# Fills of a long rest counted at full clock, and later loads in halves, in a linear-attention and MoE kernel

## The chip, the core and the metric

The kernel runs on one core of one Trainium2 chip. The metric is the device time of one execution in microseconds (us). Before the change three executions took 614.2, 611.24 and 614.52 us, with a median of 614.2 us.

## What is computed

A delta-rule attention over 768 time steps (4 batches, 8 heads, head size 48) feeds a gated two-layer product with no nonlinearity but the product of its two halves. `w_a` and `w_b` are 384 x 1536, `w_out` is 1536 x 384, and 3072 tokens go through them:

```python
for t in range(S):
    y[:, :, t] = einsum('bhd,bhde->bhe', q[:, :, t], state)
    v_old = einsum('bhde,bhd->bhe', state, k_n[:, :, t])
    state = state + beta[:, :, t] * einsum('bhd,bhe->bhde', k_n[:, :, t], v[:, :, t] - v_old)
x = y.transpose(0, 2, 1, 3).reshape(B * S, H * D)
out = ((x @ w_a) * (x @ w_b)) @ w_out
```

## The kernel before

**Tiling.** The 768 steps are 24 chunks of 32. Four chunks are a group: `prep` loads the chunks' rows, forms norms and the 32 x 32 products of keys and queries, `solve` inverts a triangular system for each head on VectorE (pairs of a multiply into `tmp` and a subtraction from `b`), and `steps` takes each chunk through the state: products named W and X (only where the inverse is made in two halves, group 0), K, U, A and the state's update S. Two chunks give one token block `s` of 256 tokens, which goes through the MoE product in twelve units, one for each block of 128 of the 1536 columns (`moe`, `moe_out`). The first two token blocks use float32 weights (`FULL = 2`), the other ten use float16 pairs.

**Weights.** The twelve weight blocks come packed as 64-bit words, 1152 KB each, by `load(b, "w")` on SyncE's queue. `decode(b)` turns one into float32 with three VectorE instructions of 128 x 1152. Blocks 0, 1 and 2 are loaded at the start. The rest, along with the raw rows (`r`, 1024 KB for two chunks, into `rawb` or `late`), the keys (`k`, `knb`) and values (`v`, `vnb`, 384 KB each), come after the first attention output of chunk 1. The buffers of the packed blocks are `late`, two halves of `stage`, and for blocks 3 to 5 a part of `wt` that is not yet used.

**How later loads are held back.** `over` is a list of one-element places. Once chunk 1's `u` is computed, each load first gets a one-element copy on GpSimd, from the place two entries back in `over` into the buffer that the load will fill. The copy cannot run before the load two back has landed, and the load cannot be issued before the copy. So two loads are in flight. The list takes loads until it has `THROTTLE` entries, 18 before. Later loads are issued as soon as their buffer is free.

**What sets the order.** Nothing is in the order in which it is written: `Plan` records every instruction as an operation, `link` finds the dependences, and `pack` lays out each engine's program with a price for each instruction, a due time for TensorE's work (`slot`, `when`), a model of TensorE's clock, and one of how its instructions are fetched. Every engine then runs its own program strictly in that order.

**Fills.** Where `pack` sees TensorE resting it adds matmuls on constants into a spare bank, whose result nobody reads, so that the clock stays up. In a rest over `LONG` (4 us) they are four-pass float32 matmuls of 128 x 512 (`self.idle[1]`, `ones`), after up to 40 tiny ones (`burn`), otherwise bfloat16 ones (`self.idle[0]`, `wide`). Before the change a fill was counted at double length where the model took the clock to be low, and in a long rest none was placed in its last 1.5 us (`SLACK`). In the profile the tiny ones are line 528, the other fills line 532, and everything else of the plan is line 541.

Of the kernel before, what the change touches and what calls it, by code (L numbers as in the profile page):

```python
# [12 lines left out]
F32 = mybir.dt.float32  # L13
F32R = mybir.dt.float32r
F16 = mybir.dt.float16
I32 = mybir.dt.int32
# [6 lines left out]
B, H, S, D = 4, 8, 768, 48  # L23
# [3 lines left out]
P = 128  # L27
# [22 lines left out]
def slot(c, piece):  # L50
    if piece == "G" and c < 4:
        v = -30 + 0.1 * c
    elif c < 2:
        v = {
            0: {"W": -20, "X": -19, "U": -17, "A": -13.1, "S": 1.0},
            1: {"W": -15.2, "X": -14, "K": -15, "Q": -11.1, "U": -13, "A": -11, "S": 2.0},
        }[c].get(piece, -30)
    elif c < 4 and piece != "G":
        v = {
            2: {"W": 2.5, "X": 3.2, "K": 3.8, "U": 4.6, "S": 5.2, "A": 5.8},  # L60
            3: {"W": 6.2, "X": 6.8, "K": 7.4, "U": 8.2, "A": 9.0, "S": 9.8},
        }[c].get(piece, -30)
    elif piece == "G":
        v = 5.0 + 2.2 * (c - 4) if c < 8 else finish(c // 4 * 4 - 4 + c % 4 // 2) - 0.5 + 0.1 * (c % 2)
    else:
        v = finish(c) - {"W": 7, "X": 6.5, "K": 5.5, "U": 4.0, "S": 3, "A": 1.5}[piece]
    return when(v)
# [3 lines left out]
LAG = 2  # L71
THROTTLE = 18
PADS, WARM = 40, 4
# [11 lines left out]
class Plan:  # L85
# [93 lines left out]
    def price(eng, name, outs, ins, kw):  # L179
        out = outs[0]  # L180
# [17 lines left out]
        if eng == "ACT":  # L198
            extra = 93.0 * (hasattr(kw.get("scale"), "tensor") + ("accum_out" in kw))
            if name == "copy" and out.dtype == F16 and wide and wide[0].dtype == F16 and out.shape[0] == 32:  # L200
                extra += 105.0
            if name == "copy" and psum and out.shape[0] == 32 and len(out.shape) == 4:
                extra += 110.0
            if name == "copy" and wide and not psum and len(wide[0].shape) == 3 and abs(wide[0].ap[-1][0]) > 4:
                extra += 225.0
            return (50 if psum else 93) + n / 1.2 + extra
        if eng == "DVE":
            speed, extra = 1.0, 61.0 * (n > 1 and any(a.shape[-1] == 1 and len(a.shape) == 2 for a in ins))
            if name == "tensor_reduce":
                n = 1  # L210
                for d in ins[0].shape[1:]:
                    n *= d
            elif name == "tensor_copy" and out.dtype == F16 and wide and wide[0].dtype == F16:
                speed, extra = 4.0, 95.0
            elif name.startswith("tensor_scalar") and not psum:
                speed = 2.0
            elif name == "memset":
                speed = 1.0 if out.dtype == F32 else 2.0
            elif name == "reciprocal":
                extra = 167.0  # L220
            return (66 + n / speed) / 0.96 + extra
# [92 lines left out]
    def pack(self, pri, back=False):  # L314
# [18 lines left out]
        while len(done) < n:  # L333
# [66 lines left out]
            if e == "PE" and not back:  # L400

                if kept and t > self.SINCE:
                    f = max(free[e], self.SINCE)
                    wide = t - f > self.LONG
                    stop_, burn, many = t - self.SLACK * wide, 0, 0

                    def spend(f, many, words, brief):
                        nonlocal until, warm, use, pos, edge, come, then
                        while True:
                            while until <= f:  # L410
                                warm = use > 0.43 * self.WINDOW if warm else use > 0.75 * self.WINDOW
                                use, until = 0.0, until + self.WINDOW
                            idle.words, idle.dur = words, brief if warm else 2 * brief
                            step = self.stall(idle, f, pos, edge, come, then)
# [6 lines left out]
                    if wide:  # L421
# [8 lines left out]
                        else:  # L430
                            burn = 0
                        many = spend(f, 0, 4, 871.0)
                    else:
                        many = spend(f, 0, 2, 218.0)
                    fill[i] = burn, many, wide
                while until <= t:
# [37 lines left out]

    START, MOVE = 900.0, (1100.0, 400.0)
    BLOCK, EDGE, FETCH, BUSY, FIRST, AHEAD, STALL, PEEK = 256, 193, 4100.0, 2500.0, 1000.0, 30, 250.0, 2
    SINCE, UNTIL, LONG, SLACK = 10000.0, 40e3, 4000.0, 1500.0
    ENTER, LEAVE, STICK = 210.0, 10.0, 15e3
# [43 lines left out]
    def issue(self, tc):  # L522
        with tc.manual_schedule():
            for i in self.order():
                burn, many, wide = self.fill.get(i, (0, 0, False))
                for n in range(burn):
# [3 lines left out]
                    )  # L530
                for _ in range(many):
                    self.nc.tensor.matmul(
                        self.pool[-1],
                        self.idle[wide],
                        self.idle[wide].unsqueeze(1).broadcast_to([P, 4, P]),
                        start=True,
# [8 lines left out]
def tile_kernel(ctx, tc, kqt, kqs, kn, vn, beta, w, masks, picks, out):  # L545
# [268 lines left out]

    def goal(c, what):
        if what == "w":
            a = place(c).bitcast(F32)
        elif what == "t":
            a = turned(c)
        elif what == "r":  # L820
            return rawp(c)[0:1, 0, 0:1]
        else:
            return (knp if what == "k" else vnp)(c)[0:1, 0, 0:1]
        return a[0:1, 0:1]

    def load(c, what):
# [3 lines left out]
        if over and what != "s" and len(over) < THROTTLE:  # L830
            dst = goal(c, what)
            G.tensor_copy(dst, over[max(0, len(over) - 2)])
            over.append(dst)
        plan.behind = set(hold)
# [694 lines left out]
```

## Time and profile before

| | |
|---|---|
| three executions | 614.2, 611.24, 614.52 us |
| the profiled execution | 614.43 us, of which the profile's span is 612.7 us |
| TensorE busy (matmuls) | 595.0 us, 97% of the span |
| VectorE, ScalarE, GpSimd busy | 404.4, 302.1, 35.5 us |
| moved by DMA | 46.46 MB, 44.85 MB of it on SyncE's queue |
| chain that ended last | 72% TensorE, 18% VectorE, 6% ScalarE |

The profile is one execution. PE is TensorE's matmuls, PEld its weight loads, DVE VectorE, ACT ScalarE, POOL GpSimd, SPq the issue of a DMA by SyncE. A row of the timeline has the start, the time taken, engine, line, operation, the tiles (out<-in), the shape and the count, and in brackets the idle time of the engine before it with what ended that. A float32 matmul shows as two instructions, so x12 is one unit's six. PEclk is the share of the full TensorE clock that was granted.

### The profile page before, as it was taken

The numbers are of one execution on the slowest core, as the hardware profiler recorded it, in microseconds if no ns is written. First come the engines' busy times: TensorE is split into PE (matmuls) and PEld (weight loads), VectorE is DVE, ScalarE is ACT, GpSimd is POOL, SyncE is SP. The second block draws the span as 40 slices with busy tenths as digits, with TensorE's granted clock in tenths as the row PEclk, the third lists the DMA queues.
The fourth block names the chain that finished last, engine by engine and source line by source line (L and its number), as shares of the span: only waits on it lengthen the run. The fifth ranks groups of instructions, "written<-read, shape, count | busy, mean of one in ns | idle before, by whom it ended". The sixth has DMA issues, their size and how long they took to land.

```text
span 612.7 us, 25247 instructions
## 1 busy us (share of the span) xinstructions
PE 595.0 (97%) x11465; PEld 466.7 (76%) x11465; DVE 404.4 (66%) x1093; ACT 302.1 (49%) x756; POOL 35.5 (6%) x49
## 2 busy tenths in 40 slices
PE   7699998999989999999999999999999999999997
PEld 4477776777768787877787778787777778777875
DVE  5869886998899845699653996553995344244222
ACT  4212323598763753564655357445356545535322
POOL 1012230001100100000101000101000000000000
PEclk9889999999999999999999999999999999999999
DMA  6718698000411204203013013010000000000000
GB/s 219 270 67 320 229 349 292 28 0 3 154 60 53 71 7 149 59 21 129 4 59 122 4 33 118 3 33 24 4 27 3 3 28 2 3 27 3 27 1 26
DMA packets 11931, 46.46 MB, mean 76 GB/s; under 512 B 1328, under 2 KB 4784, under 8 KB 8752
## 3 DMA queue, kind: packets, MB, share of 16 engines
q1 hardware_dynamic: 11824, 44.85, 20.8%
q8 instruction: 89, 1.46, 1.0%
q14 instruction: 18, 0.15, 0.1%
HBM read 40.13 MB, written 4.72 MB: 73 GB/s over the span
## 4 chain that ended last, share of the span: by engine, by line
PE 72%; DVE 18%; ACT 6%; issue 2%; DMA 1%; SPq 0%; ACTq 0%
PE bank L541 60%; PE duo L541 10%; DVE b L541 6%; DVE tmp L541 4%; PE S_ps L541 3%; ACT wt L541 2%; DVE g L541 2%; DVE wt L541 1%; ACT sqf L541 1%; DMA rawb<-in_kqt 1%; DVE ghl L541 1%; DVE f L541 1%; ACT a L541 1%; DVE n L541 1%; ACT sqy L541 1%
## 5 line engine op out<-in xcount | busy, mean ns | idle before, releaser
L541 PE MATMUL bank<-xb,wt 128*128 128x256 f16 (+1 forms) x1800 | 247.3, 291 | 2.9 <-issue 2.5
L541 PEld LDWEIGHTS <-wt 128*128 128x128 f16 x2160 | 208.1, 98 | 35.8 <-issue 1.0
L541 DVE TENSOR_TENSOR g<-bank,a 128x256 f32<-128x256 f32 x144 | 60.4, 420 | 125.3 <-ACT a L541 124.3
L541 PE MATMUL bank<-wt,ghl 128*128 128x384 f16 x720 | 136.6, 326 | 0.0
L541 ACT ACTIVATE a<-bank,gs 128x256 f32<-128x256 f32 x120 | 56.8, 473 | 119.1 <-PE bank L541 118.7
L541 PEld LDWEIGHTS <-ghl 128*128 128x128 f16 x720 | 67.6, 98 | 35.1 <-issue 0.4
L541 ACT CAST ghl<-g 128x256 f16<-128x256 f32 x120 | 48.3, 403 | 59.3 <-DVE g L541 58.7
L541 PE MATMUL bank<-stage,wt 128*128 128x256 f16 x648 | 76.7, 273 | 0.0
L541 DVE TENSOR_TENSOR ghl<-g,ghl 128x256 f16<-128x256 f32 x120 | 51.2, 427 | 33.8 <-ACT ghl L541 33.3
L541 PEld LDWEIGHTS bank<-xb,wt 128*128 128x128 f32 x288 | 53.4, 190 | 13.6 <-issue 3.1
L541 DVE TENSOR_TENSOR b<-b,tmp 128x31 f32<-128x31 f32 (+20 forms) x170 | 56.3, 331 | 3.4
L541 DVE TENSOR_TENSOR tmp<-b,b 128x31 f32<-128x31 f32 (+20 forms) x170 | 56.2, 331 | 3.3
L541 ACT COPY y<-duo 32x384 f32<-32x384 f32 x88 | 41.4, 470 | 2.5 <-PE duo L541 1.4
L541 PE MATMUL bank<-wt,g 128*128 128x384 f32 x96 | 37.5, 502 | 0.0
L541 DVE TENSOR_TENSOR f<-vnb,duo 128x768 f32<-128x768 f32 (+1 forms) x23 | 21.4, 929 | 5.8 <-issue 4.2
L541 POOL TENSOR_TENSOR vnb<-vnb,nm 128x384 f32<-128x384 f32 x20 | 17.8, 910 | 125.2 <-DMA vnb<-in_vn 104.8
L541 ACT COPY u<-duo 128x768 f32<-128x768 f32 (+1 forms) x23 | 18.1, 785 | 10.7 <-PE duo L541 10.2
L541 PEld LDWEIGHTS duo<-sh,rawb 48*64 48x64 f32 x1152 | 18.4, 134 | 5.9 <-issue 4.2
L541 ACT ACTIVATE sqy<-y 128x96 f32<-128x96 f32 x80 | 22.3, 278 | 0.9
L541 ACT COPY a<-bank 128x256 f32<-128x256 f32 x24 | 8.9, 369 | 26.4 <-PE bank L541 26.3
L541 PEld LDWEIGHTS duo<-f,tt 32*32 32x32 f32 x1408 | 16.4, 105 | 6.9 <-issue 3.6
L541 PEld LDWEIGHTS bank<-wt,g 128*128 128x128 f32 x96 | 16.9, 189 | 6.0
(156 smaller groups left out, 617.4 us busy)
## 6 DMA issues: line engine op xcount, KB each, us to landing
rawb<-in_kqt SPq DMA_DIRECT2D x10, 1024.0 KB, 5.2
stage<-in_w SPq DMA_DIRECT2D x6, 1152.0 KB, 7.3
vnb<-in_vn SPq DMA_DIRECT2D x12, 384.0 KB, 4.6
out<-ob SPq DMA_DIRECT2D x24, 192.0 KB, 1.9
knb<-in_kn SPq DMA_DIRECT2D x10, 384.0 KB, 3.9
stage<-in_kqs SPq DMA_DIRECT2D x8, 448.0 KB, 3.8
late<-in_w SPq DMA_DIRECT2D x3, 1152.0 KB, 5.8
wt<-in_w SPq DMA_DIRECT2D x3, 1152.0 KB, 6.7
```

The source lines that it names most:

```text
L541: fn(*(self.place(a, lease) for a in args), **{k: self.place(a, lease) for k, a in kw.items()})
```

## The change

It has three parts. In a long rest the fills are now counted at one length whatever the modelled clock, they may reach to 0.3 us before the next work, and a remainder is given to short fills; short rests keep 150 ns free. The loads that `over` holds back come, for weights and raw rows, as two DMAs of half the columns, each half with its own copy on GpSimd and its own entry in `over`, and the list goes up to 33 entries, so that two halves are in flight. And some numbers of the planner change: two prices, one due time, one DMA constant.

```diff
@@ -58,7 +58,7 @@
     elif c < 4 and piece != "G":
         v = {
             2: {"W": 2.5, "X": 3.2, "K": 3.8, "U": 4.6, "S": 5.2, "A": 5.8},
-            3: {"W": 6.2, "X": 6.8, "K": 7.4, "U": 8.2, "A": 9.0, "S": 9.8},
+            3: {"W": 6.2, "X": 6.8, "K": 7.4, "U": 8.2, "A": 9.0, "S": 10.4},
         }[c].get(piece, -30)
     elif piece == "G":
         v = 5.0 + 2.2 * (c - 4) if c < 8 else finish(c // 4 * 4 - 4 + c % 4 // 2) - 0.5 + 0.1 * (c % 2)
@@ -69,7 +69,7 @@
 
 EARLY = [(0, "k"), (0, "b"), (2, "k"), (0, "r"), (2, "r")], [(0, "m"), (0, "v"), (2, "v"), (0, "w"), (1, "w")], [(2, "w")], [(3, "w"), (4, "w"), (4, "k"), (4, "r"), (5, "w")], [(6, "w"), (6, "k"), (6, "r"), (7, "w"), (4, "v"), (6, "v"), (8, "w")]
 LAG = 2
-THROTTLE = 18
+THROTTLE = 33
 PADS, WARM = 40, 4
 LEAD = 4
 
@@ -199,13 +199,15 @@
             extra = 93.0 * (hasattr(kw.get("scale"), "tensor") + ("accum_out" in kw))
             if name == "copy" and out.dtype == F16 and wide and wide[0].dtype == F16 and out.shape[0] == 32:
                 extra += 105.0
-            if name == "copy" and psum and out.shape[0] == 32 and len(out.shape) == 4:
+            if name == "copy" and psum and out.shape[0] == 32:
                 extra += 110.0
             if name == "copy" and wide and not psum and len(wide[0].shape) == 3 and abs(wide[0].ap[-1][0]) > 4:
                 extra += 225.0
             return (50 if psum else 93) + n / 1.2 + extra
         if eng == "DVE":
             speed, extra = 1.0, 61.0 * (n > 1 and any(a.shape[-1] == 1 and len(a.shape) == 2 for a in ins))
+            if name == "tensor_mul" and psum and len(out.shape) > 2:
+                extra += 150.0
             if name == "tensor_reduce":
                 n = 1
                 for d in ins[0].shape[1:]:
@@ -402,7 +404,7 @@
                 if kept and t > self.SINCE:
                     f = max(free[e], self.SINCE)
                     wide = t - f > self.LONG
-                    stop_, burn, many = t - self.SLACK * wide, 0, 0
+                    stop_, burn, many = t - (self.SLACK if wide else 150.0), 0, 0
 
                     def spend(f, many, words, brief):
                         nonlocal until, warm, use, pos, edge, come, then
@@ -410,7 +412,7 @@
                             while until <= f:
                                 warm = use > 0.43 * self.WINDOW if warm else use > 0.75 * self.WINDOW
                                 use, until = 0.0, until + self.WINDOW
-                            idle.words, idle.dur = words, brief if warm else 2 * brief
+                            idle.words, idle.dur = words, brief if warm or wide else 2 * brief
                             step = self.stall(idle, f, pos, edge, come, then)
                             if f + step[0] + idle.dur > stop_:
                                 return many
@@ -430,9 +432,11 @@
                         else:
                             burn = 0
                         many = spend(f, 0, 4, 871.0)
+                        fine = int((stop_ - f - 871.0 * many) // 218.0)
+                        pos += 2 * fine
                     else:
-                        many = spend(f, 0, 2, 218.0)
-                    fill[i] = burn, many, wide
+                        many, fine = 0, spend(f, 0, 2, 218.0)
+                    fill[i] = burn, many, fine
                 while until <= t:
                     warm = use > 0.43 * self.WINDOW if warm else use > 0.75 * self.WINDOW
                     use, until = 0.0, until + self.WINDOW
@@ -472,9 +476,9 @@
                     heapq.heappush(wait[ops[k].eng], (ready[k], k))
         return at, stop, done, max(stop), ({b: h[0] for b, h in held.items()}, fill)
 
-    START, MOVE = 900.0, (1100.0, 400.0)
+    START, MOVE = 900.0, (1100.0, 1000.0)
     BLOCK, EDGE, FETCH, BUSY, FIRST, AHEAD, STALL, PEEK = 256, 193, 4100.0, 2500.0, 1000.0, 30, 250.0, 2
-    SINCE, UNTIL, LONG, SLACK = 10000.0, 40e3, 4000.0, 1500.0
+    SINCE, UNTIL, LONG, SLACK = 10000.0, 40e3, 4000.0, 300.0
     ENTER, LEAVE, STICK = 210.0, 10.0, 15e3
     CALM = 40e3
     SOON = 2000.0
@@ -522,17 +526,17 @@
     def issue(self, tc):
         with tc.manual_schedule():
             for i in self.order():
-                burn, many, wide = self.fill.get(i, (0, 0, False))
+                burn, many, fine = self.fill.get(i, (0, 0, 0))
                 for n in range(burn):
                     x = slice(32 * (n % 4), 32 * (n % 4) + 32)
                     self.nc.tensor.matmul(
                         self.pool[-1][x, 0:2], self.tiny[x], self.tiny[x, 0:2], start=True, stop=True, skip_group_check=True
                     )
-                for _ in range(many):
+                for x in [self.idle[1]] * many + [self.idle[0]] * fine:
                     self.nc.tensor.matmul(
                         self.pool[-1],
-                        self.idle[wide],
-                        self.idle[wide].unsqueeze(1).broadcast_to([P, 4, P]),
+                        x,
+                        x.unsqueeze(1).broadcast_to([P, 4, P]),
                         start=True,
                         stop=True,
                         skip_group_check=True,
@@ -812,25 +816,28 @@
 
     loaded, whole = set(), set()
 
-    def goal(c, what):
+    def goal(c, what, half=0):
         if what == "w":
-            a = place(c).bitcast(F32)
-        elif what == "t":
-            a = turned(c)
-        elif what == "r":
-            return rawp(c)[0:1, 0, 0:1]
-        else:
-            return (knp if what == "k" else vnp)(c)[0:1, 0, 0:1]
-        return a[0:1, 0:1]
+            return place(c)[:, half * WD :].bitcast(F32)[0:1, 0:1]
+        if what == "r":
+            return rawp(c)[0:1, half, 0:1]
+        return (turned(c) if what == "t" else (knp if what == "k" else vnp)(c)[:, 0])[0:1, 0:1]
 
     def load(c, what):
         if (c, what) in loaded:
             return
         loaded.add((c, what))
         if over and what != "s" and len(over) < THROTTLE:
-            dst = goal(c, what)
-            G.tensor_copy(dst, over[max(0, len(over) - 2)])
-            over.append(dst)
+            for i in range(2 if what in "wr" else 1):
+                dst = goal(c, what, i)
+                G.tensor_copy(dst, over[max(0, len(over) - 2)])
+                over.append(dst)
+                if what == "w":
+                    SP.dma_start(place(c)[:, i * WD : (i + 1) * WD], w[c].bitcast(I32)[:, i * WD : (i + 1) * WD])
+                elif what == "r":
+                    SP.dma_start(rawp(c)[:, i], kqt[c // 2][:, 1024 * i : 1024 * i + 1024])
+            if what in "wr":
+                return
         plan.behind = set(hold)
         if what == "w":
             SP.dma_start(place(c), w[c].bitcast(I32))
```

The first place is TensorE's program around the rest in which VectorE solves group 0 (`solve`, before the product W of chunk 0). `ones` and `wide` are the fills' constants. Before:

```order
L541 MATMUL bank_61<-rawb 32x64 x32
L541 MATMUL bank_62<-rawb 32x64 x32
L528 MATMUL bank_64<-ones 32x2 x25
L532 MATMUL bank_64<-ones 128x512 x5
L541 MATMUL bank_63<-b_3_70,wt 64x16 x16
L541 MATMUL bank_61<-b_3_70,mk 128x256
```

The same place after the change:

```order
L545 MATMUL bank_62<-rawb 32x64 x32
L532 MATMUL bank_64<-ones 32x2 x23
L536 MATMUL bank_64<-ones 128x512 x9
L545 MATMUL bank_63<-b_3_70,wt 64x16 x16
L545 MATMUL bank_61<-b_3_70,mk 128x256
```

Nine long fills stand where five stood. The work on both sides is the same; of short fills, three now stand ahead of `bank_62<-rawb`, and before the first K product with `u` of chunk 0 there are two where there were three.

The second place is SyncE's queue from the first held-back load (weight block 3) to block 9. Before:

```order
L541 DMA wt<-in_w 128x2304 x2
L541 DMA sel<-in_picks 128x132
L541 DMA knb<-in_kn 128x768
L541 DMA rawb<-in_kqt 128x2048
L541 DMA wt<-in_w 128x2304
L541 DMA late<-in_w 128x2304
L541 DMA knb<-in_kn 128x768
L541 DMA rawb<-in_kqt 128x2048
L541 DMA stage<-in_w 128x2304
L541 DMA vnb<-in_vn 128x768 x2
L541 DMA stage<-in_w 128x2304
L541 DMA late<-in_w 128x2304
```

After:

```order
L545 DMA wt<-in_w 128x1152 x2
L545 DMA sel<-in_picks 128x132
L545 DMA wt<-in_w 128x1152 x2
L545 DMA knb<-in_kn 128x768
L545 DMA rawb<-in_kqt 128x1024 x2
L545 DMA wt<-in_w 128x1152 x2
L545 DMA late<-in_w 128x1152 x2
L545 DMA knb<-in_kn 128x768
L545 DMA rawb<-in_kqt 128x1024 x2
L545 DMA stage<-in_w 128x1152 x2
L545 DMA vnb<-in_vn 128x768 x2
L545 DMA stage<-in_w 128x1152 x2
```

The loads keep their order down to block 9. On GpSimd, four products of the values with their norms (`vnb,nm`) stood behind the copy for block 8; now two stand between the copies for its two halves, and two behind the second. Each weight block and each pair of raw rows is two entries. The first `stage` row is block 7, the one behind `vnb` block 8.

The third place is TensorE's program around unit 7 of token block 0 (its six matmuls `bank<-xb,wt`), whose weights are block 7. `wt,g` are the output products of earlier units, and `sh_74,rawb` is chunk 3's K product. Before:

```order
L541 MATMUL bank_61<-wt,g_98 128x384
L541 MATMUL bank_64<-xb,wt 128x256 x6
L541 MATMUL bank_63<-wt,g_99 128x384
L541 MATMUL bank_61<-wt,g_99 128x384
L541 MATMUL duo<-sh_74,rawb 64x48 x32
```

After:

```order
L545 MATMUL bank_63<-wt,g_99 128x384
L545 MATMUL bank_61<-wt,g_99 128x384
...
L545 MATMUL bank_63<-wt,g_97 128x384
L545 MATMUL bank_64<-xb,wt 128x256 x6
L545 MATMUL duo<-sh_74,rawb 64x48 x32
L545 MATMUL bank_61<-wt,g_97 128x384
```

Three output products that stood behind unit 7 now stand ahead of it. Unit 8 moves back in the same way: ahead of it now stand also the second `wt,g_97` product, the two `wt,g_98` products, chunk 3's U product (`f_71,tt_82`) and A product (`u_72,at_76`).

## The prediction

> **What bounds the kernel now.** I read the page, then the busy time by stretches, then the timeline from 14 to 45 us and around the weights' arrival, and the changed order. The page:
>
> ```profile
> span 612.7 us, 25247 instructions
> PE 595.0 (97%) x11465; PEld 466.7 (76%) x11465; DVE 404.4 (66%) x1093; ACT 302.1 (49%) x756; POOL 35.5 (6%) x49
> ```
>
> TensorE is idle for 17.7 us in all, so whatever is gained is idle time closed or work done at a higher clock. The stretches (duration; busy time of PE, PEld, DVE, ACT, POOL; granted clock; DMA share; GB/s) say where:
>
> ```profile
> 26.00:27.00 1.00, 0.85 (x16) 0.88 (x18) 1.00 (x3) 0.00 (x0) 0.00 (x0) 0.55 0.68 286
> 30.00:35.00 5.00, 5.00 (x71) 3.80 (x71) 2.53 (x4) 0.76 (x2) 0.00 (x0) 0.50 0.02 5
> 36.00:37.00 1.00, 1.00 (x15) 0.78 (x14) 0.29 (x1) 0.00 (x0) 0.00 (x0) 0.83 0.00 0
> 37.00:40.00 3.00, 3.00 (x126) 2.40 (x126) 1.91 (x3) 0.48 (x1) 0.00 (x0) 1.00 0.03 5
> 90.00:100.00 10.00, 9.98 (x232) 7.43 (x230) 9.43 (x12) 5.29 (x12) 0.17 (x1) 1.00 1.00 386
> 100.00:105.00 5.00, 2.48 (x70) 1.99 (x70) 0.58 (x2) 0.37 (x1) 0.18 (x1) 1.00 0.72 203
> 160.00:200.00 40.00, 37.97 (x868) 29.66 (x871) 36.03 (x102) 23.72 (x59) 1.93 (x2) 1.00 0.24 86
> ```
>
> From 26 to about 36.3 us the clock is halved. At 100 us, after ten microseconds in which the DMA engines were full, TensorE stands for 2.5 us; another 2.0 us are idle between 160 and 200. The rows around the low clock:
>
> ```profile
> 16.87 4.56 PE L532 MATMUL bank<-ones 128*128 128x512 f32 x10
> 26.15 1.89 PE L541 MATMUL bank<-b,wt 64*64 64x16 f32 x32 [4.72 <-DVE b L541]
> 29.79 1.89 PE L541 MATMUL bank<-b,wt 64*64 64x16 f32 x32
> 31.52 1.92 PE L541 MATMUL duo<-vnb,wt 64*64 64x48 f32 x32
> 33.38 1.46 PE L532 MATMUL bank<-wide 128*128 128x512 bf16 x3
> 33.49 0.48 ACT L541 COPY wt<-duo 128x384 f32<-128x384 f32 x1 [1.48 <-PE duo L541]
> 34.77 1.84 PE L541 MATMUL duo<-wt 64*64 64x48 f32 x32
> 38.22 1.13 PE L541 MATMUL bank<-wt 64*64 64x48 f32 x32
> 40.34 0.48 ACT L541 COPY u<-duo 128x384 f32<-128x384 f32 x1 [0.45 <-DVE wt L541]
> 41.06 1.10 PE L541 MATMUL bank<-u,wt 64*64 64x48 f32 x32
> 42.09 1.47 PE L532 MATMUL bank<-wide 128*128 128x512 bf16 x6
> 43.40 1.95 PE L541 MATMUL bank<-xb,wt 128*128 128x256 f32 x8
> ```
>
> Five long fills end at 21.43, and TensorE rests for 4.72 us until VectorE's solve releases the product W at 26.15. Then chunks 0 and 1 go through a chain of small products at half clock, and the first MoE unit starts at 43.40.
>
> **The head.** A long fill takes 4.56/5 = 0.91 us, so nine from 16.87 end at 25.1: they don't delay W, and the rest is 1 us instead of 4.72. I take the clock to stay up, since it stayed at 1.00 across the stop of 2.5 us at 100 us. Four products lie on the chain at half clock, 1.89, 1.89, 1.92 and 1.84 us. The same kind takes 1.13 and 1.10 at full clock, so each gives back 0.75 to 0.8: 3.1 us. Also the three fills at 33.38, slow at half clock, hold the product behind them: its input is ready at 33.97, another such step (40.82 to 41.06) shows 0.24 us from ScalarE to TensorE, so it could start at 34.21 and starts at 34.77. At full clock a short fill takes 1.47/6 = 0.25, two of them 0.5, which ends before the copy does: 0.56 us more. That is 3.7. VectorE's weight decode stands between the steps in program order and may take some back, so I count **-3.5**; bounds 0 (the clock falls anyway) and -3.7. From the first MoE unit on TensorE is nearly dense, so this passes to the end unless something is late.
>
> The Trainium skill, "TensorE: Matmul & The Clock Gate" (the HAM clock gate), says that the clock returns to full after one busy window of about 3.4 us. The trace disagrees: it stays halved about 10.2 us with TensorE busy from 26.15 on. By the page the head would give only a third, some 1.2 us; by the rows 3.5, and the rows decide. The page also says that the windows run free of the kernel, which no view here shows, but 611.24 beside 614.5 would fit an execution of before whose rest fell luckily.
>
> **The loads.** The page's list of DMAs (KB each, median us from issue to landing), GpSimd's groups from 40 to 105 us, and the first held-back issue:
>
> ```profile
> rawb<-in_kqt SPq DMA_DIRECT2D x10, 1024.0 KB, 5.2
> knb<-in_kn SPq DMA_DIRECT2D x10, 384.0 KB, 3.9
> stage<-in_kqs SPq DMA_DIRECT2D x8, 448.0 KB, 3.8
> L541 POOL TENSOR_TENSOR vnb<-vnb,nm 128x384 f32<-128x384 f32 x4 | 4.0, 1029 | 0.3 <-DMA vnb<-in_vn 0.3
> L541 POOL COPY wt<-knb 1x1 f32<-1x1 f32 x1 | 1.2, 1246 | 1.0 <-DMA knb<-in_kn 1.0
> L541 POOL COPY knb<-wt 1x1 f32<-1x1 f32 x2 | 0.4, 176 | 8.2 <-DMA wt<-in_w 8.2
> 42.11 0.99 SPq L541 DMA_DIRECT2D wt<-in_w  x2
> ```
>
> A half weight block has 576 KB. Between 448 KB (3.8) and 1024 KB (5.2) that gives 4.1 us by a straight line; half the raw rows (512 KB) 4.0, keys 3.9. A one-element copy on GpSimd takes 0.18 to 1.25, say 0.65, and semaphores about 0.15. So an entry of `over` needs 4.9 us from the landing two back to its own, and two entries run side by side. Up to block 7 there are 16 entries (blocks 3 to 7, two pairs of raw rows, two of keys): 8 rounds of 4.9 less the first turn of 0.8, 38.4 us. Before, those loads took from 42.11 to 74.64, 32.5 us. What was saved in bytes in flight is lost in turns. Where it meets TensorE:
>
> ```profile
> 74.64 0.76 DVE L541 TENSOR_SCALAR wt<-stage 128x1152 int32<-128x1152 int32 x1 [1.80 <-DMA stage<-in_w]
> 77.48 2.22 DVE L541 SCALAR_TENSOR_TENSOR wt<-stage,wt 128x1152 int32<-128x1152 int32 x1
> 80.97 2.75 PE L541 MATMUL bank<-xb,wt 128*128 128x256 f32 x12
> 82.79 0.76 DVE L541 TENSOR_SCALAR wt<-stage 128x1152 int32<-128x1152 int32 x1 [1.57 <-DMA stage<-in_w]
> 85.20 1.35 DVE L541 SCALAR_TENSOR_TENSOR wt<-stage,wt 128x1152 int32<-128x1152 int32 x1
> 86.92 1.24 PE L541 MATMUL bank<-xb,wt 128*128 128x256 f32 x5
> ```
>
> VectorE waited for blocks 7 and 8, decoded them by 79.70 and 86.55 (5.06 and 3.76 us), and their units began at 80.97 and 86.92: before had 1.3 and 0.4 us to spare. After, the first load issues at 42.11 - 3.5 = 38.6, block 7 lands at 77.0, is decoded at 82.1. TensorE comes to unit 7 at 80.97 - 3.5 plus the three output products now ahead of it, 0.7 us each:
>
> ```profile
> 96.90 1.56 PE L541 MATMUL bank<-wt,g 128*128 128x384 f32 x4
> 98.29 0.29 PE L541 MATMUL bank<-wide,sqw 128*128 128x1 bf16 x6
> 63.28 0.81 PE duo L541 x64
> 102.52 1.56 PE L541 MATMUL bank<-xb,wt 128*128 128x256 f32 x6 [2.53 <-issue]
> ```
>
> (two of them from 96.90 to 98.29; the third row is from the chain of waits), so 79.6, and waits 2.5. For block 8 two more rounds (9.8) and one pair of GpSimd's products between its copies (two of 1.03, part of it overlapped: 0.8) give 87.6, decoded at 91.4. TensorE would be there at 86.92 - 3.5 + 4.6 = 88.0, the 4.6 being three output products (2.1), a U and an A product (0.81 each) and three groups of six norms (0.29 each). The wait to that point is **+3.4** in all. Everything in TensorE's queue stands behind it. Blocks 9 to 11 come a round apart (4.9), their units as far or farther, so I add nothing. Bounds: with every copy at 0.18 and 3.8 a load a round takes 4.1, block 7 lands at 71.1, and there is no wait. With 5.2, a whole load's time, and copies of 0.95, the round takes 6.3 and unit 7 alone waits 13. 576 KB is near the 448 KB row, so I stay near the low end.
>
> The Trainium skill, "DMA: Bandwidth & Descriptors" (Measured), advises transfers of 1 MiB and more, against this change, and puts a DMA at 2.0 us plus its bytes at 436 GB/s. By that, an estimate, half a block takes 3.4, a round 4.2, and the wait would be nil; rows of this trace are slower than that at every size, so the sum goes by them.
>
> **The stop at 100 us** (the row of 102.52 above) ends on "issue", on nothing that the profile records, just when the DMA engines come free; I read it as TensorE's next instructions arriving late behind queued loads. Then smaller and fewer bytes in flight, with the list reaching 33 entries and so past block 11, should remove it: **-2.5**. It can also stay (0) or come elsewhere (+2.5). The Trainium skill, "Runtime: NRT & Kernel Launch" (Instruction fetch mechanics), holds that fetching blocks of instructions is mostly hidden; by it this stop is something else and stays, which is the third rival below.
>
> The due time, two prices and the DMA constant only reorder work; dense TensorE work hides that. Without that cover it is bounded by the 2.0 us idle between 160 and 200, either way; I take 0.
>
> **The sum.** From the profiled execution, 614.43 - 3.5 + 3.4 - 2.5 = 611.8; the median of before is 0.2 lower, so 611.6.
>
> **Rivals.**
> - *The halves arrive in time*: rounds of 4.1 to 4.3. For: some copies take 0.18. Against: VectorE's work lengthens others to 1.25. No wait: 614.2 - 6.0 = 608.2.
> - *The halves are the bound*, slower than before: ten rounds lead to block 8, so each 0.1 us a round is 1 us. Before is reached when the wait is 6.0 us, at rounds of 5.2; from 5.5 it is slower by over 3 us. At 5.6 the wait is 10.4: 614.2 - 6.0 + 10.4 = 618.6. For: the rows of 1024 KB show 5.2, and a copy can take 1.25. Against: so slow a round needs both at once.
> - *The stop at 100 stays or moves*, for more DMAs are issued and TensorE's fetches meet them all the same: 614.1.
> - *The change doesn't do what it says*: the clock falls despite the fills, since 1 us of rest and slow small products are left. Then -3.5 goes: 615.1. Against: the stop of 2.5 us at 100 us, with the clock at 1.00.
>
> **How the numbers follow.** The forecast gets 0.40, halves in time 0.25, halves as the bound 0.15, the stop 0.12, no clock gained 0.08. A measurement of this kernel can tell about 0.5%, 3.1 us, from no change: below 611.1 is faster, above 617.3 slower. Faster holds the second case and about 0.15 of the forecast's own spread (waits of 2 to 5 us: 610.2 to 613.2): 0.40. Slower is the bound case, 0.15. The rest, 0.45, is within. The range from 607.5 to 616.5 leaves out the bound case and the far ends of the costs.
>
> **What would show it.** Right: a granted clock of 1.00 from 26 to 37 us, the four products at 1.1 us, the first unit near 39.9, VectorE waiting on `in_w` for block 7 till about 77 and TensorE waiting on VectorE `wt` at units 7 and 8 for some 3.4 us together, no "issue" gap near 100. Wrong: a half landing in under 3.7 us or over 4.6, a first unit after 41, or new "issue" gaps.

## The result, and the profile after

Six executions of the changed kernel took 619.8 to 627.65 us, with a median of 622.77; beside them on the same chip before has a median of 613.56 (611.24 to 616.76). The ratio is 1.0145, with a 95% interval from 1.0102 to 1.0189. The forecast was 611.6 with a range up to 616.5, so it was wrong, and on the other side: the kernel is slower. The profiled execution took 627.65 us, the longest of the six, so its waits are nearer to the worst than to the middle. The page:

```profile
span 625.9 us, 25317 instructions
PE 606.7 (97%) x11469; PEld 473.5 (76%) x11469; DVE 404.4 (65%) x1093; ACT 301.0 (48%) x756; POOL 38.9 (6%) x64
```

The share of 97% has not moved. That is no comfort: TensorE's busy time itself grew by 11.7 us with four instructions more. Of that, 3.4 us are the longer fills at the head (7.99 us against 4.56); the rest fits work done at a lower clock. The stretches (duration; busy time of PE, PEld, DVE, ACT, POOL; granted clock; DMA share; GB/s):

```profile
26.00:27.00 1.00, 0.27 (x11) 0.40 (x11) 1.00 (x3) 0.00 (x0) 0.00 (x0) 1.00 1.00 424
30.00:35.00 5.00, 5.00 (x74) 4.07 (x74) 2.22 (x4) 0.76 (x2) 0.00 (x0) 0.50 0.02 5
43.00:86.00 43.00, 39.09 (x778) 29.59 (x775) 29.91 (x46) 11.58 (x23) 8.09 (x17) 0.92 0.65 210
45.00:130.00 85.00, 75.21 (x1468) 57.21 (x1469) 59.70 (x95) 22.99 (x50) 16.72 (x33) 0.92 0.67 216
76.00:83.00 7.00, 4.84 (x73) 3.64 (x74) 5.42 (x15) 0.97 (x4) 0.68 (x3) 0.52 0.74 233
120.00:127.00 7.00, 5.15 (x12) 4.18 (x13) 5.13 (x12) 0.02 (x1) 0.35 (x2) 0.55 0.64 194
130.00:600.00 470.00, 468.11 (x8956) 371.49 (x8955) 309.82 (x917) 256.33 (x657) 17.90 (x21) 1.00 0.13 42
```

The same wide stretches before:

```profile
43.00:86.00 43.00, 43.00 (x959) 33.23 (x957) 37.39 (x55) 11.34 (x24) 12.21 (x16) 1.00 0.79 285
45.00:130.00 85.00, 82.47 (x1540) 63.70 (x1539) 72.94 (x142) 33.89 (x80) 12.73 (x19) 1.00 0.62 224
130.00:600.00 470.00, 467.10 (x8985) 371.00 (x8985) 298.82 (x878) 250.33 (x635) 17.57 (x20) 1.00 0.12 40
```

Read three things here. At 26 us the clock now stands at 1.00, but from 30 to 35 it is 0.50 as before: it still falls, later. From 43 to 86 us, while the held-back loads come in, the DMA engines are busy 65% instead of 79% and move 210 GB/s instead of 285. And TensorE, dense in that stretch before, is idle 3.9 us in it, with low clock at 76 and again at 120.

That accounts for the 13.2 us between the two profiled executions (627.65 against 614.43). From 45 to 130 us TensorE idles 9.8 us against 2.5, +7.3. In the two low stretches it is busy 4.8 and 5.2 us at about half clock, which costs half of that, some 5.0. The first unit starts 1.6 us later (44.98 below, against 43.40). From 130 us on, 1.0 us less is idle. Sum: 12.9.

TensorE's timeline at the head:

```profile
17.46 7.99 PE L536 MATMUL bank<-ones 128*128 128x512 f32 x18
26.73 1.11 PE L545 MATMUL bank<-b,wt 64*64 64x16 f32 x32 [1.28 <-DVE b L545]
...
31.46 1.92 PE L545 MATMUL duo<-vnb,wt 64*64 64x48 f32 x31
...
34.28 1.95 PE L545 MATMUL duo<-wt 64*64 64x48 f32 x32
...
44.98 1.35 PE L545 MATMUL bank<-xb,wt 128*128 128x256 f32 x5
```

The nine long fills (x18, two instructions each) do what was said of them: the rest is 1.28 us instead of 4.72, and the first product, W, takes 1.11 us. But the next small products take 1.92 and 1.95, as before.

The first held-back issue on SyncE's queue, and the page's sizes and landing times (KB each, median us from issue to landing):

```profile
43.03 0.81 SPq L545 DMA_DIRECT2D wt<-in_w  x2
```

```profile
stage<-in_w SPq DMA_DIRECT2D x8, 576.0 KB, 5.0
wt<-in_w SPq DMA_DIRECT2D x6, 576.0 KB, 4.5
rawb<-in_kqt SPq DMA_DIRECT2D x6, 512.0 KB, 4.5
late<-in_w SPq DMA_DIRECT2D x4, 576.0 KB, 5.1
```

VectorE's waits from 40 to 125 us, in total, times and longest:

```profile
DVE wt L545 <- DMA stage<-in_w: 5.8, 3, 3.5
DVE wt L545 <- DMA late<-in_w: 4.2, 2, 3.7
DVE wt L545 <- DMA wt<-in_w: 3.2, 1, 3.2
```

VectorE waits 13.2 us for weights (before: 3.4, for blocks 7 and 8). TensorE's stops behind that, in its timeline, then two of VectorE's waits with what follows them:

```profile
78.16 2.04 PE L545 MATMUL bank<-xb,wt 128*128 128x256 f32 x4 [3.90 <-DVE wt L545]
...
109.39 1.35 PE L545 MATMUL bank<-xb,wt 128*128 128x256 f32 x5 [0.84 <-issue]
...
121.85 8.22 PE L545 MATMUL bank<-xb,wt 128*128 128x256 f32 x24 [2.82 <-DVE g L545]
```

```profile
86.55 0.76 DVE L545 TENSOR_SCALAR wt<-stage 128x1152 int32<-128x1152 int32 x1 [0.52 <-DMA stage<-in_w]
...
117.81 0.76 DVE L545 TENSOR_SCALAR wt<-stage 128x1152 int32<-128x1152 int32 x1 [3.48 <-DMA stage<-in_w]
...
120.10 1.36 DVE L545 SCALAR_TENSOR_TENSOR wt<-stage,wt 128x1152 int32<-128x1152 int32 x1
121.38 0.42 DVE L545 TENSOR_TENSOR g<-bank,a 128x256 f32<-128x256 f32 x1
```

Block 7's decode starts at 86.55 us, 43.5 after the first held-back issue, where before needed 32.5. The long stops belong to blocks 6 (78.16) and 11 (121.85). In the last, the wait is named after `g`, but `g` only stood in VectorE's program behind a decode that waited 3.48 us for its block: one late load holds a unit's weights and another unit's products. The only stop on "issue" left near 100 is the 0.84 us at 109.39.

Block 11 was not late by the rounds alone. The second row below is the issue of its second half, which VectorE could decode from 117.81 on, 9.3 us later. It shared the DMA engines with a whole load of raw rows (1024 KB, the first row), for which GpSimd has no copy, so the list doesn't hold it back. That this made the half late fits its neighbours' 4.5 to 5.1 us, but was not tried alone:

```profile
106.53 1.82 SPq L545 DMA_DIRECT2D late<-in_kqt  x1
108.55 0.33 SPq L545 DMA_DIRECT2D stage<-in_w  x1
```

### The profile page after: what moved, and what is told of

Read it like the earlier page. It is cut to its first block, busy times and chain, and to the rows that moved or that the text cites. A ratio compares the mean times of both kernels' runs of the same rounds, so it can differ in the third digit from the quotient of the medians.

```text
span 625.9 us, 25317 instructions
## 1 busy us (share of the span) xinstructions
PE 606.7 (97%) x11469; PEld 473.5 (76%) x11469; DVE 404.4 (65%) x1093; ACT 301.0 (48%) x756; POOL 38.9 (6%) x64
## 3 DMA queue, kind: packets, MB, share of 16 engines
HBM read 40.13 MB, written 4.72 MB: 72 GB/s over the span
## 4 chain that ended last, share of the span: by engine, by line
PE 74%; DMA 11%; DVE 7%; ACT 4%; POOL 1%; issue 1%; SPq 0%; POOLq 0%; DVEq 0%
PE bank L545 61%; PE duo L545 10%; DMA stage<-in_w 4%; PE S_ps L545 2%; DVE wt L545 2%; DVE b L545 2%; DMA wt<-in_w 2%; DMA rawb<-in_kqt 2%; DMA late<-in_w 2%; ACT wt L545 2%; ACT sqf L545 1%; DVE tmp L545 1%; DMA vnb<-in_vn 1%; DMA knb<-in_kn 1%; DVE ss L545 1%
## 5 line engine op out<-in xcount | busy, mean ns | idle before, releaser
L545 PE MATMUL bank<-xb,wt 128*128 128x256 f16 (+1 forms) x1800 | 251.8, 294 | 8.2 <-DVE wt L545 4.4
L545 PEld LDWEIGHTS bank<-xb,wt 128*128 128x128 f32 x288 | 56.4, 201 | 21.3 <-issue 5.7
```

The lines of the kernel that those rows point to most:

```text
L545: fn(*(self.place(a, lease) for a in args), **{k: self.place(a, lease) for k, a in kw.items()})
```

## The experiments

Theory A: the load queue is the bound, because two halves in flight keep too few bytes moving. Rivals: the fills do harm (B); the planner's numbers do harm (C). Beside it, two steps of the prediction could be tried alone: that a closed rest holds the clock, and that the stop at 100 us comes from the short list. Each ratio is against before on the same chip. Of each edit the lines that matter are shown, and `...` stands for lines left out.

**Fills alone.** Before with only the change to the fills; loads and numbers as before.

```diff
-                    stop_, burn, many = t - self.SLACK * wide, 0, 0
+                    stop_, burn, many = t - (self.SLACK if wide else 150.0), 0, 0
...
-                            idle.words, idle.dur = words, brief if warm else 2 * brief
+                            idle.words, idle.dur = words, brief if warm or wide else 2 * brief
...
+                        fine = int((stop_ - f - 871.0 * many) // 218.0)
...
```

> The fills' rules of the change alone; loads, list and prices as before. Theory (the rest of 1.3 us that is left, with small products on both sides, still lets the clock fall, only later): the clock is halved for 10 us or more from about 28 us, the first MoE unit comes at 43 to 45 us as before, 612 to 615 us. Rival, the prediction's own (nine fills hold the clock): 1.00 from 26 to 37 us, first unit near 40, about 610 us.

It took 616.09 us, ratio 1.0049 [1.0014, 1.0084]: no gain. In its profile the first unit starts at 42.21, 1.2 us earlier than before; the clock was low at 16.5 to 23.3 us, so the long fills took 10.24 us, and full through the chain. So the expected fall in the chain didn't come in this execution. What it won at the head it lost at 100 us, where the stop is still there and the clock is at half from 101.9 to 105.3 us:

```profile
101.08 1.78 PE L543 MATMUL bank<-xb,wt 128*128 128x256 f32 x5 [2.66 <-issue]
```

**The rest closed.** The same with five more short fills behind the long ones.

```diff
-                    fill[i] = burn, many, fine
+                    fill[i] = burn, many, fine + 5 * wide
```

> As fills_only, with five more short fills (0.25 us each) behind the nine long ones, so that TensorE rests for under 0.3 us before the first W. Theory (what lets the clock fall is the remainder of the rest): the clock stays at 1.00 to 40 us, the four small products take 1.1 us each, the first unit starts near 40, about 610 us. Rival (the small products count for too little by themselves): the clock falls all the same one window later, and the time is that of before, 612 to 615 us.

It took 619.59 us, 1.0116 [1.0074, 1.0158]. TensorE's timeline, then a stretch:

```profile
26.15 1.24 PE L534 MATMUL bank<-wide 128*128 128x512 bf16 x5
...
40.75 2.86 PE L543 MATMUL bank<-xb,wt 128*128 128x256 f32 x12
...
99.49 0.27 PE L543 MATMUL bank<-wide,sqw 128*128 128x1 bf16 x4 [3.24 <-issue]
```

```profile
98.00:104.00 6.00, 4.51 (x24) 2.90 (x28) 0.00 (x0) 0.90 (x2) 0.17 (x1) 0.50 0.51 127
```

In this execution the clock held, and the first unit came at 40.75, 2.65 us earlier: the size of the head's term was right, its condition is the open point. The stop at 100 is still there, longer (3.24), and in it the clock falls (at 98.0 us, until 104.8). This was the shortest of four executions (616.35, with a mean clock of 0.993); the other three, 618.78 to 622.09, had mean clocks of 0.980 to 0.985, so they were low for longer. Where they were low isn't recorded.

**The halves alone.** Before with the halving and the list of 33, without fills or numbers.

```diff
-THROTTLE = 18
+THROTTLE = 33
...
+            for i in range(2 if what in "wr" else 1):
+                dst = goal(c, what, i)
+                G.tensor_copy(dst, over[max(0, len(over) - 2)])
+                over.append(dst)
...
```

> The loads in halves and the list of 33 entries alone; fills, prices and due time as before. Theory (a round of landing and turn of about 5.5 us for two half loads bounds the decode): VectorE and TensorE wait for the weights from unit 6 on, block 7 lands some 43 us after the first held-back issue, 620 to 624 us. Rival (the new prices and the due time moved TensorE's units badly, the halves are harmless): 612 to 616 us.

627.48 us, 1.0242 [1.0213, 1.0271]: the halves, with the longer list that goes with them, cost 15 us alone, more than the whole change. Block 7 landed at 85.2, 42.5 us after the first held-back issue. B and C fall as main causes.

**Three halves in flight, and four.** The changed kernel with one number changed.

```diff
-                G.tensor_copy(dst, over[max(0, len(over) - 2)])
+                G.tensor_copy(dst, over[max(0, len(over) - 3)])
```

> The changed kernel with each half waiting for the landing three entries back, not two: three halves in flight. Theory (the bound is the round's fixed time, not bandwidth): block 7 lands 30 to 33 us after the first held-back issue, the waits at units 6 to 11 fall from 9.7 us to 2 or less, 612 to 615 us. Rival (half-size packets move fewer bytes a second, or GpSimd's copies are the bound): block 7 lands 40 us or more after it, 619 us or more.

> The changed kernel with each half waiting for the landing four entries back: the bytes in flight are those of two whole loads. Theory (what costs is the time of a round, shared by two small loads): block 7 lands 31 to 34 us after the first held-back issue, 611 to 615 us, like the kernel with whole loads. Rival (more DMAs, copies and smaller packets cost by themselves): block 7 later than 36 us, 617 us or more.

Three: 619.05 us, 1.0111 [1.0067, 1.0155], with block 7 landed 35.7 us after the first issue. Four: 620.26, 1.0121 [1.0066, 1.0176], with block 7 landed after 29.0 us, earlier than ever, and still no gain. The stretch from 43 to 86 us of three, and of four, shows the loads faster and faster:

```profile
43.00:86.00 43.00, 38.18 (x763) 29.68 (x760) 33.43 (x48) 11.09 (x23) 13.15 (x24) 0.92 0.76 254
```

```profile
43.00:86.00 43.00, 42.99 (x966) 32.49 (x963) 39.11 (x57) 11.83 (x24) 18.29 (x26) 1.00 0.90 320
```

So each has a stop of another kind. With three, VectorE stands for 3.92 us with block 7's decode, the next `g` is behind it, and TensorE waits for that (VectorE's rows, then TensorE's):

```profile
78.70 0.76 DVE L545 TENSOR_SCALAR wt<-stage 128x1152 int32<-128x1152 int32 x1 [3.92 <-DMA stage<-in_w]
...
79.48 0.42 DVE L545 TENSOR_TENSOR g<-bank,a 128x256 f32<-128x256 f32 x1
```

```profile
79.95 1.05 PE L545 MATMUL bank<-b,tt 32*32 32x16 f32 x64 [4.81 <-DVE g L545]
```

With four VectorE waits for one load only (1.59 us, for block 9), and `g` stands behind decodes that run early:

```profile
88.43 2.82 DVE L545 SCALAR_TENSOR_TENSOR wt<-stage,wt 128x1152 int32<-128x1152 int32 x2
...
91.96 2.82 DVE L545 SCALAR_TENSOR_TENSOR wt<-stage,wt 128x1152 int32<-128x1152 int32 x2
94.70 0.42 DVE L545 TENSOR_TENSOR g<-bank,a 128x256 f32<-128x256 f32 x1
```

```profile
95.17 0.30 PE L545 MATMUL bank<-wide,sqw 128*128 128x1 bf16 x6 [5.28 <-DVE g L545]
```

VectorE decodes without a gap from 84.91 to 94.78, while ScalarE had `g`'s other factor ready at 89.06: the program has three decodes in a row ahead of `g`. My theory expected the time of whole loads once the bytes were there; it holds for the loads and fails for the time. Why the planner orders this program so was not tried.

**Whole loads.** The changed kernel with the halving undone; the list of 21 reaches past block 11 as 33 halves did.

```diff
-THROTTLE = 33
+THROTTLE = 21
...
-            for i in range(2 if what in "wr" else 1):
-                dst = goal(c, what, i)
...
+            dst = goal(c, what)
+            G.tensor_copy(dst, over[max(0, len(over) - 2)])
...
```

> The changed kernel with whole loads again, two in flight, and a list that covers the same loads (21 entries): only the halving is undone. Theory (the halving is what costs, by its rounds): block 7 lands 32 to 34 us after the first held-back issue, and the time is 611 to 616 us, 7 to 11 below the changed kernel. Rival (the planner's new numbers and the longer list cost half of it): 617 us or more.

611.6 us, 0.9953 [0.9931, 0.9975], 11.2 us under the changed kernel's median. The stretches of 43 and 45 us:

```profile
43.00:86.00 43.00, 42.99 (x926) 33.20 (x924) 38.61 (x54) 11.78 (x24) 8.78 (x16) 0.98 0.80 291
45.00:130.00 85.00, 84.85 (x1551) 65.43 (x1549) 79.73 (x152) 34.84 (x82) 11.36 (x22) 1.00 0.64 228
```

TensorE idles 0.15 us in 85, against 9.79, and VectorE has no wait for weights in the stretch. Halving is the cause, seen from both sides: doing it alone costs 15, undoing it alone gives 11. Yet the first unit starts at 45.9 here, for the clock was low from 30.9 to 44.5.

**The planner's numbers alone.** Before with the two prices, the due time and the DMA constant.

```diff
-            3: {"W": 6.2, "X": 6.8, "K": 7.4, "U": 8.2, "A": 9.0, "S": 9.8},
+            3: {"W": 6.2, "X": 6.8, "K": 7.4, "U": 8.2, "A": 9.0, "S": 10.4},
...
-    START, MOVE = 900.0, (1100.0, 400.0)
+    START, MOVE = 900.0, (1100.0, 1000.0)
```

> The kernel before with the two prices, the due time and the DMA constant of the change alone. Theory (they only reorder work that covers itself): within 2 us of before, 611 to 615 us. Rival (they are a cost of their own): 616 us or more.

612.12 us, 0.9969 [0.9943, 0.9994], a gain of 0.3%. The idle time that the prediction named as its bound is closed in its profile, from 2.0 us to none, and in those of the three other versions that have these numbers and whole loads:

```profile
160.00:200.00 40.00, 40.00 (x790) 31.22 (x789) 35.39 (x102) 21.42 (x55) 0.83 (x1) 1.00 0.20 68
```

**A longer list alone, three times.** `THROTTLE` alone, in before (24), in the version with the rest closed (24), and in the planner's numbers alone (21).

```diff
-THROTTLE = 18
+THROTTLE = 24
```

> The kernel before with a list of 24 entries, so that the loads behind block 11 are held back too, two whole loads in flight. Theory (TensorE's stop at 100 us is its instruction fetch behind six loads that nothing holds back): no issue gap over 1 us between 90 and 110 us, and 609 to 611 us. Rival (the stop is not the loads' doing): the gap of 2.5 us stays, time as before.

> The kernel with the rest closed by nine long and five short fills, with the list of 24 entries as well. Theory (the head's gain was lost in that kernel because TensorE came earlier to the same stop near 100 us and its clock then fell): clock at 1.00 from 26 to 110 us, first unit near 40.5, no stop, 606 to 609 us. Rival (the head's gain does not last for other reasons): 612 us or more.

> The kernel with whole loads and the list of 21 entries, the new prices and due time, but the fills' rules of before. Theory (the new fills bring nothing that lasts, since the clock falls one or two windows later): within 1.5 us of the kernel with whole loads and the new fills, 611 to 613 us. Rival (they hold the clock in most executions): 2 us or more above it.

Before with 24: 613.68 us, 0.9982 [0.9953, 1.0011], no clear change in time. But its stretch at 98 us has no stop:

```profile
98.00:104.00 6.00, 6.00 (x151) 4.67 (x150) 5.49 (x8) 3.57 (x8) 1.25 (x1) 1.00 0.26 82
```

The profiled execution gave the gain back at the head, low for 20.5 us (23.7 to 44.2), with a first unit at 46.3. The closed rest with 24: 613.89, 1.0005 [0.9970, 1.0040], where the list of 18 had 1.0116, with no stop at 100; yet the clock fell there from 30.5 to 40.8 us, although TensorE had not rested for more than 0.21 us since 15.8. TensorE's rows where it falls:

```profile
30.23 0.41 PE L543 MATMUL bank<-b,wt 64*64 64x16 f32 x9 [0.21 <-issue]
30.49 1.89 PE L543 MATMUL duo<-vnb,wt 64*64 64x48 f32 x32
```

The numbers with 21: 610.97, 0.9956 [0.9920, 0.9991], as fast as whole loads with the new fills (611.6). So with whole loads the longer list removes the stop, and the new fills by themselves bring nothing that lasts. One thing doesn't fit the list as the only cause: with the numbers alone and the old list the stop is down to 0.72 us already (at 102.22).

**Fills inside the chain.** If the fall comes from the small products, not from the rest, fills between them should prevent it. Whole loads as above, with three short fills ahead of two products of chunk 0, an X product and U.

```diff
                 burn, many, fine = self.fill.get(i, (0, 0, 0))
+                o = self.ops[i]
+                if o.eng == "PE" and (o.due == slot(0, "U") or o.due == slot(0, "X") and len(o.calls) == 1):
+                    fine += 3
```

> The kernel with whole loads (611.6 us) with three short fills more ahead of chunk 0's X product and of each U product of chunks 0 and 1 that the planner finds, 0.25 us each on the chain. Theory (after the rest, the small products by themselves keep TensorE below what holds its clock): the clock stays at 1.00 from 26 to 45 us, the small products take 1.1 us, the first unit starts at 41 to 43 us, 608 to 611 us. Rival (what lets it fall is idle time, or chance): it falls as in the kernel without them, 612 to 614 us.

607.74 us, 0.9907 [0.9877, 0.9937]: faster than both kernels. Its clock row in 40 slices, and TensorE at the head:

```profile
PEclk9999999999999999999999999999999999999999
```

```profile
26.75 1.11 PE L548 MATMUL bank<-b,wt 64*64 64x16 f32 x32 [0.51 <-DVE b L548]
27.79 0.82 PE L539 MATMUL bank<-wide 128*128 128x512 bf16 x3
...
31.09 0.82 PE L539 MATMUL bank<-wide 128*128 128x512 bf16 x3
...
41.44 2.86 PE L548 MATMUL bank<-xb,wt 128*128 128x256 f32 x12
```

The clock never falls between 5.8 and 603 us, and eight of ten executions have a mean clock of 0.999 or 1.000. Six short fills, 1.6 us of work that nobody reads, bring 3.9 us against the median of whole loads without them (0.5% by the two ratios). All ten executions of whole loads without them have a mean clock of 0.985 to 0.989. One rival is left: without the fills the profile has a stop of 1.06 us on "issue" that ends at 31.00, about where the clock falls (30.9), and with them it has none. Whether the fills act by filling the chain or by moving that stop was not tried apart; in the closed rest with 24 the clock fell behind a rest of only 0.21 us.

**The same with halves.** Does the halving still cost as much when the clock holds? The changed kernel with these six fills.

```diff
+                o = self.ops[i]
+                if o.eng == "PE" and (o.due == slot(0, "U") or o.due == slot(0, "X") and len(o.calls) == 1):
+                    fine += 3
```

> The changed kernel (halves, two in flight, list 33) with the three short fills at two places of chunk 0's chain that kept the clock at 1.00 in the version with whole loads (607.7). It splits the 11 us that whole loads gave back into two causes. Theory (the turns of the halves are the bound, whatever the clock at the start): the first unit moves to about 41.5, but so do the loads, by some 2.5 us; block 7 lands 43 us after the first held-back issue, near 84, TensorE then waits for the decodes of blocks 7 to 11 by some 9 to 13 us in all (more than the 9.7 of the changed kernel, since TensorE comes earlier), the clock falls for one or two windows behind those waits, and the time is 616 to 621. Rival (the slow start is what made the waits expensive; with the clock held the halves are hidden): waits under 5 us, 608 to 612.

620.14 us, 1.0103 [1.0073, 1.0132], inside the expected 616 to 621. The first unit starts at 40.40, and the waits are:

```profile
45.00:130.00 85.00, 76.11 (x1382) 57.94 (x1382) 62.87 (x118) 26.64 (x60) 15.46 (x33) 0.98 0.67 216
```

TensorE idles 8.9 us, at a clock of 0.98. The halving costs 12.4 us against whole loads with the same fills (620.14 less 607.74), and a full clock at the start doesn't hide it. Coming earlier at unit 5 (69.66 us) TensorE waits 3.86 us there, in a place where the changed kernel had no wait: what the head gains, the loads take.

## Why the prediction was wrong

**The step that failed** is the load's landing time. "576 KB is near the 448 KB row, so I stay near the low end": the straight line gave 4.1 us, the halves land in 4.5 to 5.1. The 16 entries took 43.5 us, so a round took (43.5 + 0.8)/8 = 5.5 us, not 4.9. All of the 0.6 more lies in the landing: along the eight entries that lead to block 7's second half the trace has landings of 4.79 us on the mean and turns of 0.67, against some 4.05 and 0.8 counted. The rival "the halves are the bound" named this mechanism, and the point from which it is slower (rounds of 5.5); it got 0.15. The clue was in the rows used: a straight line through two medians took loads for independent, though their time also depends on what else is moving (with four in flight a half takes 5.3 to 6.0 us). Both signs of being wrong that the prediction named came: a half over 4.6 us, and a first unit after 41. The quantity that needed a forecast was the rate with two halves in flight: 210 GB/s here, 285 before.

**The size of the wait** follows from that round as far as unit 8. By the rival's own rule, 1 us for each 0.1 us of a round, rounds of 5.5 turn the +3.4 into 9.4. In the profile unit 8 starts at 102.06, 15.1 us after before's 86.92; without the later head (1.6) and the products now ahead of it (4.6) that is 9.0, of which 6.0 are idle time of TensorE and some 2.4 the low clock from 76 us on. What the sum didn't have is the place and what comes after. The first long wait is at unit 6 (3.90 us), and units 7 and 8, where I expected it, wait 0.50 and nothing. Behind unit 8 I added nothing, "their units as far or farther", yet TensorE stands 2.82 us before unit 11. I counted what a late block does to its own unit; VectorE's program has the next `g` behind the waiting decode, as at 117.81 to 121.38. And with each of the two long waits came a low clock, some 5 us more in the profiled execution, which no term held.

**The head (-3.5)** failed by its condition, and the fourth rival, given 0.08, is what happened. The fills filled the rest, but the clock fell among the small products, and the first unit moved to 44.98 instead of 39.9. The price of the four products was right: where the clock held, units began at 40.4 to 41.4, and at 42.2 with the fills alone, whose long fills had run at half clock. My evidence, a clock of 1.00 across a stop of 2.5 us at 100, was one instance; the closed rest and the fills alone show the clock falling at such a stop.

The Trainium skill, "TensorE: Matmul & The Clock Gate" (the HAM clock gate), tells of a free-running window of about 3.4 us. The lengths of the low stretches agree: 3.41, 6.83, 10.24, 13.65, 17.07 and 20.48 us are multiples of 3.41. Its rule that one busy window brings the clock back doesn't hold for this work: in before with the list of 24 TensorE is busy from 26.24 us on, and the clock low until 44.18.

**The stop at 100 us (-2.5)** was right for whole loads and in part for this kernel. In the three pairs of versions that differ in the list alone, the longest stop on "issue" between 85 and 110 us goes from 2.53 to 0.67 us, from 3.24 to 0.50 and from 0.72 to 0.35. That the list removes it there is shown. With halves some of it is left in spite of the list: 0.84 us at 109.39 in this kernel, 1.86 at 101.04 with the halves alone, 1.72 at 104.57 with the fills inside the chain. That it works by TensorE's instructions arriving late behind queued loads was argued and stays so; in the trace of before, one packet of instructions (16 KB) moves between 95 and 103 us, and it starts at 99.91, just as TensorE stands, which fits, but the trace doesn't say whose instructions they are. The gain was covered by the other terms.

**The planner's numbers (0, within 2.0)** were right within their bound: 0.3% faster.

**Size, or bytes in flight.** From 43 to 86 us two halves in flight moved 210 GB/s, three 254, four 320, two whole loads 291: with more bytes in flight the same halves move faster than whole loads. The Trainium skill, "DMA: Bandwidth & Descriptors" (Measured), advises transfers of 1 MiB and more, and the slower two halves agree; the four halves don't, so in these runs the bytes in flight decide, not the size of one DMA. The Trainium skill, in the same page's section "Anatomy of one DMA — SWDGE (gpsimd) path", gives the formula 2.0 us plus bytes at 436 GB/s, fitted on DMAs by that path, while these go by SyncE's queue. It gives an estimate of 3.4 us for a half; 4.5 to 5.1 was measured with two in flight. That rows of before are slower than it "at every size" holds for the loads, not for the 192 KB stores: 1.9 us, where it gives an estimate of 2.5.

## What to carry to other kernels

When a change splits transfers and keeps the number in flight, forecast the bytes in flight and the rate they give, then walk the schedule with that rate; here block 7 came 43.5 us after the first held-back issue, where 38.4 was forecast and before needed 32.5. Price a late input by everything that stands behind the waiting instruction in its engine's program, on every engine, and add the clock that falls while TensorE waits. And to hold TensorE's clock through a chain of small products, try a few wide fills between them: here they held it in eight of ten executions by the mean clock, where closing the rest ahead of them held it in one profile and not in another.

## What the runs showed of the hardware that was not expected

- The clock falls while TensorE is busy by the profile: in the closed rest with the list of 24 TensorE was busy 14.51 of the 14.72 us ahead of the fall at 30.54, and then 10.24 of 10.24 us at 0.50, with products of 64x16, 64x48 and 32x16. With three short fills (0.82 us) at two places between such products the clock stayed at 1.00 (607.74 us against 611.6 without them).
- The same program's clock falls or holds by execution: with the rest closed, mean clocks of four executions were 0.980 to 0.993.
- Four halves in flight moved more (320 GB/s) than two whole loads (291), although each took longer to land: 5.3 to 6.0 us by the page's medians, against 4.5 to 5.1 with two.
